# A transformer block on one core: the opening's layer-norm root taken from ScalarE, its first block worked in halves, and its splits in another order

## The chip, the cores and the metric

The kernel runs on one core of a Trainium2 chip. The core has a matrix engine (TensorE, PE in the profile, with its weight loads shown as PEld), a vector engine (VectorE, DVE), a scalar engine (ScalarE, ACT), GpSimd (POOL), and SyncE (SP), which issues most of the transfers. Each engine works through its own instructions in the order in which the program issues them; engines wait for one another through semaphores. The metric is the time of one execution on the device in microseconds.

## The reference

A pre-normed attention layer with 32 query heads on one shared key and value head, followed by a bilinear feed-forward layer, on 2048 rows of width 576 in float32:

```python
B, S, D, H = 1, 2048, 576, 32;  Dh = D // H          # Dh = 18, F = 4608
x = A_x
h = x + attention(_layernorm(x), wq, wk, wv, wo)      # softmax(q k^T * Dh**-0.5) v, then @ wo
n = _layernorm(h)
h2 = h + ((n @ w_gate) * (n @ w_up)) @ w_down         # no nonlinearity on either branch

def _layernorm(x, axis=-1, eps=1e-5):
    m = jnp.mean(x, axis=axis, keepdims=True)
    v = jnp.var(x, axis=axis, keepdims=True)
    return (x - m) / jnp.sqrt(v + eps)
```

## The kernel before

The 2048 rows are worked in four blocks of 512, each of four tiles of 128 rows. To come near float32, most products are made from a high and a low part of each operand: `split` casts a value to the matrix format on one engine (the high part, usually ScalarE, line 96) and subtracts the cast from the value on VectorE (the low part, line 97). A product is then three matmuls: high by high, low by high and high by low; `passes` lists them for the five 128-row slices of the width (the fifth holds the last 64 columns twice, its lower half the low part, so it needs two).

The program has three stages. The opening, `keys_values`, normalises all of x, transposes it, and projects keys and values. Then come score and value products of block 0 (`pair` and `flush`), with the query projections of all blocks between them, and at last the feed-forward layer of each block with the next block's attention dealt in between. The order of every engine's work is written out by hand; nothing is reordered by time.

The opening, in the order of its own names:

- `stats(lo, hi)` takes mean and variance of tiles lo to hi on VectorE (`ln_stats`, lines 111 and 112: two partial statistics and their union for a tile).
- `scale(lo, hi, eng)` makes 1/sqrt(variance + 1e-5) and the negative product of it and the mean. `rstd` (lines 121 to 133) starts from an integer estimate and makes three Newton steps; block 0 does it on VectorE, blocks 1 to 3 on GpSimd, where a step has one instruction more.
- `apply(b)` writes the normalised tiles xh of a block on ScalarE (line 194), four instructions.
- `twice(eng)` copies the last 64 columns of each xh beside themselves (line 199), on GpSimd for blocks 0 and 3 and on VectorE for blocks 1 and 2.
- `turn(b)` transposes on TensorE: two PSUM tiles tr of two row tiles each, and a tail.
- `parts()` splits what has been transposed into XT: a cast and a subtraction for each of the two tr, and for the tail.
- `project(b)` multiplies XT of a block by the joint weights w_h and w_l of keys, values and the last queries (14 matmuls, line 232). The raw weights wkv and wqr come by SP's queue behind block 0's x.
- `mean`, `keys` and `bound` make the keys' high and low part kk, their largest absolute value kabs and from it a bound on the scores, which replaces the maximum in the softmax; the bound, the queries and the keys pass through memory by SP's queue (lines 255, 276, 449, 534, 540).
- `queries(0)`, taken a step at a time as `first`, projects block 0's queries (line 407 and from line 416).

The first `pair` needs kT and the loads of q with its bound. From then on the loop of `run` alternates score products, one exponential instruction on ScalarE for each (line 611) and the value products.

Of the kernel before, what the change touches and what calls it, by code (L numbers as in the profile page):

```python
# [26 lines left out]
P = 128  # L27
# [3 lines left out]
NQ = TB // P  # L31
# [26 lines left out]
class Block:  # L58
# [84 lines left out]
    def keys_values(self):  # L143

        pe, act, dve, sp, pool = self.pe, self.act, self.dve, self.sp, self.nc.gpsimd
        p0 = self.op
# [23 lines left out]
        mv = p0.tile([P, NT, 2], F32, name="mv")  # L170
        nmean, kab, kabq = (p0.tile([P, 1], F32, name=n) for n in ("nmean", "kab", "kabq"))
        kabs = p0.tile([P, NB], F32, name="kabs")
        pool.memset(nmean, 0.0)
        pool.memset(kabs, 0.0)
        rs, xhs, trs, psks, tq_last = {}, {}, [], {}, []

        def stats(lo, hi):
            for j in range(lo, hi):
                b, s = divmod(j, NQ)
                self.ln_stats(xs[b][:, s, :], mv[:, j, :], s, f"a{b}")  # L180

        def scale(lo, hi, eng):
            r = self.rstd(mv[:, lo:hi, 1], f"a{lo}", eng, hi - lo)
            n = self.lp.tile([P, hi - lo], F32, tag="n", name=f"n{lo}")
            eng.tensor_tensor(n, mv[:, lo:hi, 0], r, ALU.mult)
            eng.tensor_scalar(n, n, -1.0, None, ALU.mult)
            for j in range(lo, hi):
                rs[j] = r[:, j - lo:j - lo + 1], n[:, j - lo:j - lo + 1]

        def apply(b):  # L190
            for s in range(NQ):
                xh = xhs[s] = self.p0q.tile([P, 640], F32, tag=f"wq{1 + s // 2}_{s % 2}", name=f"xh{b}_{s}")
                r, n = rs[NQ * b + s]
                act.activation(xh[:, 0:D], xs[b][:, s, :], AF.Identity, bias=n, scale=r)

        def twice(eng, lo=0, hi=NQ):

            for s in range(lo, hi):
                eng.tensor_copy(xhs[s][:, D:], xhs[s][:, 512:D])

        def turn(b):

            tail = self.ps_m(f"trt{b}")
            for r in range(2):
                tr = self.ps_s(f"tr{b}_{r}").rearrange("p a (c q) -> p (a c) q", q=2 * P)
                for s in (2 * r, 2 * r + 1):
                    for c in range(4):
                        pe.transpose(tr[:, c, (s - 2 * r) * P:(s - 2 * r + 1) * P],
                                     xhs[s][:, c * P:(c + 1) * P], self.ident)
                trs.append((b, r, tr))  # L210
                yield
            for s in range(NQ):
                pe.transpose(tail[:, s * P:(s + 1) * P], xhs[s][:, 512:], self.ident)
                del xhs[s]
            trs.append((b, None, tail))
            yield

        def parts():

            while trs:  # L220
                b, r, tr = trs.pop(0)
                XT = self.XT[b]
                if r is None:
                    self.split_tail(XT[:, 8, :], tr)
                else:
                    sl = slice(2 * r * P, (2 * r + 2) * P)
                    self.split(XT[:, 0:4, sl], XT[:, 4:8, sl], tr)

        def project(b):
            psk = psks[b] = (self.ps_f if b % 2 else self.ps_a)(f"psk{b}")  # L230
            for i, (w, m) in enumerate(passes(w_h, w_l, self.XT[b])):
                pe.matmul(psk, w, m, start=(i == 0), stop=(i == 13))

        def mean():

            act.activation(kv[:, 0:TB], psks[0], AF.Copy, accum_out=ksum)
            dve.tensor_scalar(nmean[R_K:], ksum[R_K:], -1.0 / TB, None, ALU.mult)

        def keys(b):


            sl = slice(b * TB, (b + 1) * TB)
            kk = self.pp.tile([P, 2, TB], F32R, tag="P", name=f"kk{b}")
            act.activation(kk[:, 0], psks[b], AF.Identity, bias=nmean)

            def highest():
                dve.tensor_reduce(kabs[R_K:, b:b + 1], f32(kk[R_K:, 0]), AX.X, ALU.max, apply_absolute_value=True)

            def low():
                if b:  # L250
                    dve.tensor_copy(kv[64:96, sl], psks[b][64:96])
                dve.scalar_tensor_tensor(kk[:, 1], psks[b], nmean, f32(kk[:, 0]), ALU.add, ALU.subtract)
                del psks[b]
                for j, k in enumerate((0, 0, 1)):
                    sp.dma_start(f32(self.kT[j:3 * DH:3, sl]), f32(kk[R_K:R_K + DH, k]))
                if b:
                    store()
                    again(b)

            def store():  # L260
                rows = self.q_dram[b, HL * DH:]
                sp.dma_start(rows[:, 0:2, :], f32(kk[:R_V]))
                sp.dma_start(rows[:, 2, :], f32(kk[:R_V, 0]))

            def queries():
                if not b:
                    store()
                tq = self.qb.tile([P, TB], F32R, tag="tq", bufs=5, name=f"tql{b}")
                dve.scalar_tensor_tensor(tq[:R_V], f32(kk[:R_V, 0]), -1.0, f32(kk[:R_V, 0]), ALU.mult, ALU.max)
                tq_last.append(tq)  # L270
            return highest, low, queries
# [18 lines left out]

        first = self.queries(0)

        act.copy(w_h, wkv)
# [5 lines left out]
        pool.tensor_tensor(w_l, wkv, f32(w_h), ALU.subtract)  # L299
# [1246 lines left out]
def rows(b, c):  # L1546

    return 7 * DH if b == 0 and c < 4 else P


def drain(gen):
    for _ in gen:
        pass
# [85 lines left out]
```

## Time and profile before

| what | value |
|---|---|
| median of 3 runs | 2285.42 us (2283.07 to 2285.66) |
| profiled execution | 2286.16 us, of which the span from the first to the last instruction is 2284.4 us |
| mean granted TensorE clock | 0.999 |
| TensorE matmuls busy | 2250.6 us, 99% of the span |
| ScalarE busy | 1510.1 us, 66% |
| VectorE busy | 1272.1 us, 56% |
| GpSimd busy | 726.6 us, 32% |
| first score matmul starts | 47.62 us |

A row of the order of time gives the start, the length, the engine, the line of the code, the operation and its tiles, how many instructions were merged, and in brackets how long the engine had stood idle before it and what ended that. A row of the groups gives the line, engine, operation and shapes, the count, then busy time in total and the mean of one in nanoseconds, then the idle time before them with its releasers. The rows of the stretches are explained where they stand.

### The profile page before, as it was taken

The page shows a single profiled execution, that of the slowest core. Times are in us where ns is not written, and L with a number is a line of the kernel's source. Part 1 is how long each engine was busy: PE and PEld are TensorE (multiplying, and loading weights), DVE is VectorE, ACT ScalarE, POOL GpSimd, SP SyncE. Part 2 cuts the span into 40 slices and gives each one's busy share as a digit, 9 for nine tenths or more (in the row PEclk, how much of TensorE's full clock was granted, in tenths as well). Part 3 has the DMA queues.
Part 4 walks back from the last instruction along what each step waited for, and adds up shares of the span by engine and source line. Part 5 has one row for each costly group of instructions (what it writes and reads, how often), then busy time and mean ns, then how long its engine had stood idle before and what let it go on. Part 6 is the DMA issues. An engine that isn't in the chain of part 4 may idle for free.

```text
span 2284.4 us, 46386 instructions
## 1 busy us (share of the span) xinstructions
PE 2250.6 (99%) x17958; PEld 1635.1 (72%) x17958; DVE 1272.1 (56%) x2190; ACT 1510.1 (66%) x2052; POOL 726.6 (32%) x848
## 2 busy tenths in 40 slices
PE   7999999999999999999999999999999999999999
PEld 5333334777777777777777777767777788999999
DVE  7655635444445446454544455544444477778776
ACT  5889877767776766667676767567676724555553
POOL 5445401323333333233333333322222244222222
PEclk9999999999999999999999999999999999999999
DMA  5778853545555554645555544654343345677775
GB/s 172 232 257 294 274 195 96 160 150 164 170 168 162 169 173 142 202 155 171 163 168 167 161 163 153 193 183 138 118 128 101 106 165 172 207 244 237 233 248 171
DMA packets 199271, 407.05 MB, mean 178 GB/s; under 512 B 21342, under 2 KB 53214, under 8 KB 199046
## 3 DMA queue, kind: packets, MB, share of 16 engines
q1 hardware_dynamic: 196309, 392.78, 53.6%
q0 software_dynamic: 2736, 11.26, 1.6%
q8 instruction: 143, 2.34, 0.4%
q14 instruction: 83, 0.67, 0.1%
HBM read 317.27 MB, written 74.55 MB: 172 GB/s over the span
## 4 chain that ended last, share of the span: by engine, by line
PE 82%; DVE 1%; ACT 1%; issue 1%; POOL 1%; DMA 0%; SPq 0%; ACTq 0%; POOLq 0%; DVEq 0%
PE pg L945 22%; PE acc L615 15%; PE y L897 13%; PE s L610 9%; PE gs L1161 8%; PE yq L1126 4%; PE pu L945 3%; PE yo L741 3%; PE gu L945 2%; PE gs L1168 2%; PE y L867 1%; ACT P L611 0%; DMA out_dram<-h 0%; POOL h L908 0%; DVE ws L97 0%
## 5 line engine op out<-in xcount | busy, mean ns | idle before, releaser
L611 ACT ACTIVATE P<-s 128x1024 f32<-128x1024 f32 x1024 | 1025.6, 1027 | 277.0 <-PE s L610 198.4
L945 PE MATMUL pu<-X,ws 64*128 64x512 f32 x2565 | 694.2, 389 | 0.0
L945 PE MATMUL pg<-X,ws 64*128 64x512 f32 x2565 | 693.1, 389 | 0.1
L945 PEld LDWEIGHTS pg<-X,ws 64*128 64x128 f32 x2565 | 475.1, 185 | 70.7 <-DMA wsum<-in_wgs_dram 0.8
L615 PE MATMUL acc<-P,V 128*32 128x512 f32 x4096 | 491.3, 599 | 0.7 <-ACT P L611 0.6
L945 PEld LDWEIGHTS pu<-X,ws 64*128 64x128 f32 x2565 | 472.4, 185 | 6.9 <-ACT tmp L874 0.3
L610 PE MATMUL s<-q,kT 56*128 56x512 f32 x2048 | 443.2, 422 | 7.2 <-ACT P L611 3.7
L908 POOL TENSOR_TENSOR h<-h,tmp 128x288 f32<-128x288 f32 x306 | 238.5, 806 | 597.8 <-ACT tmp L907 596.3
L610 PEld LDWEIGHTS s<-q,kT 56*128 56x128 f32 x2048 | 201.1, 184 | 207.4 <-ACT P L611 119.8
L897 PEld LDWEIGHTS y<-wdo,room 128*128 128x128 f32 x2142 | 289.8, 188 | 43.2 <-issue 34.8
L897 PE MATMUL y<-wdo,room 128*128 128x288 f32 x2142 | 303.8, 300 | 1.3 <-DVE h L903 1.2
L615 PEld LDWEIGHTS acc<-P,V 128*32 128x32 f32 x4096 | 114.5, 109 | 247.0 <-issue 236.2
L903 DVE TENSOR_TENSOR h<-h,y 128x288 f32<-128x288 f32 x408 | 175.8, 452 | 200.5 <-PE y L897 200.3
L907 ACT COPY tmp<-y 128x288 f32<-128x288 f32 x306 | 122.0, 399 | 241.4 <-PE y L897 219.0
L976 DVE TENSOR_TENSOR hf<-pu,g 128x512 f32<-128x512 f32 x95 | 65.7, 691 | 302.6 <-ACT g L972 302.6
L96 POOL CAST ws<-wr 128x1152 fp32r<-128x1152 f32 x108 | 127.0, 1176 | 315.0 <-PE pu L945 244.7
L97 DVE TENSOR_TENSOR ws<-wr,ws 128x1152 fp32r<-128x1152 f32 x108 | 185.2, 1715 | 64.6 <-POOL ws L96 61.8
L1109 POOL TENSOR_TENSOR wsum<-wsum,wsum 128x512 f32<-128x512 f32 x72 | 99.4, 1381 | 137.8 <-DMA wsum<-in_wgs_dram 137.7
L97 DVE TENSOR_TENSOR room<-S,room 128x1024 fp32r<-128x1024 f32 x51 | 62.5, 1226 | 132.1 <-ACT room L96 132.1
L1126 PE MATMUL yq<-wdo,XW 128*128 128x288 f32 x504 | 86.0, 297 | 0.1
L945 PE MATMUL gu<-X,ws 64*128 64x512 f32 x702 | 82.0, 389 | 0.0
L748 DVE TENSOR_TENSOR h<-h,yo 128x288 f32<-128x288 f32 x154 | 63.3, 452 | 32.3 <-PE yo L741 28.5
(257 smaller groups left out, 2638.6 us busy)
## 6 DMA issues: line engine op xcount, KB each, us to landing
wdo<-wd_dram SPq DMA_DIRECT2D x492, 288.0 KB
wr<-in_wgu_dram SPq DMA_DIRECT2D x108, 576.0 KB
wsum<-in_wgs_dram SPq DMA_DIRECT2D x108, 256.0 KB
wd_dram<-wd_room SPq DMA_DIRECT2D x20, 1008.0 KB
wsum_dram<-wsum SPq DMA_DIRECT2D x72, 256.0 KB
raw<-wsum_dram SPq DMA_DIRECT2D x72, 256.0 KB
q<-q_dram SPq DMA_DIRECT2D x64, 216.0 KB
raw<-in_wgs_dram SPq DMA_DIRECT2D x54, 256.0 KB
```

The lines of the kernel that those rows point to most:

```text
L96: (copy or self.cast)(hi, src)
L97: self.dve.tensor_tensor(lo, src, f32(hi), ALU.subtract)
L610: self.pe.matmul(s_[:, i], self.kT[o:o + 56, t * P:(t + 1) * P], q[o:o + 56, pr], start=True, stop=True)
L611: self.act.activation(p_, s_, AF.Exp, scale=SCALE)
L615: self.pe.matmul(acc[32 * j:32 * j + 32, :], self.V[:, t, :], Ps[j // 2][:, j % 2, :], start=(t == 0), stop=(t == NT - 1), skip_group_chec ...
L897: pe.matmul(y[:, :HD], m[:, t * P:(t + 1) * P], k, start=(first and j == 0), stop=(j == 2), skip_group_check=True)
L903: dve.tensor_tensor(hs, hs, y[:, :HD], ALU.add)
L907: act.copy(z, y[:, :HD])
L908: pool.tensor_tensor(hs, hs, z, ALU.add)
L945: pe.matmul(ps, w[o:o + 64, wk, c], X[o:o + 64, xk, c], start=(j == 0), stop=(j == 26))
L1126: pe.matmul(y[:, :HD], A[:, k, x, t * P:(t + 1) * P], v[:, l], start=(first and z == j == 0), stop=(z == len(pairs) - 1 and j == 2), skip_ ...
L1161: pe.matmul(bank[:, g * HT:(g + 1) * HT], W[:, wk, c, g], X[:, 2 * xk + c], start=(first and g == c == wk == xk == 0), stop=(c == 1 and wk ...
```

## The change

Only the opening is changed, and the order of the matmuls inside a key projection.

- **The root.** The integer estimate and three Newton steps give way to a square root of variance + eps on ScalarE (`root`), a reciprocal of it on VectorE and one Newton step on the engine that did the work before (VectorE for block 0, GpSimd for the others). On VectorE a chain has six instructions, on GpSimd seven beside VectorE's reciprocal. A constant tile eps is set on GpSimd. After the keys of block 2, one Exp of that tile is issued on ScalarE.
- **Halves.** Block 0 takes statistics, root and scale for tiles 0 and 1, then for tiles 2 and 3; tile 0 is applied before the second root, the other three after it.
- **The weights.** w_h is cast and w_l subtracted on GpSimd; the cast of the first query weights moves on ScalarE behind block 0's casts.
- **Low parts.** `high` and `low` take the cast and the subtraction of a tr apart, so that they stand in another order among roots and reciprocals.
- **Copies.** The tail copies of blocks 1 and 2 move from VectorE to GpSimd.
- **Order.** Statistics of blocks 1 to 3 are taken at other places; `highs_first` puts the products with the high part of XT ahead of those with its low part.

```diff
+        eps = p0.tile([P, 1], F32, name="eps")
+        pool.memset(eps, 1e-5)
...
+        def root(lo, hi):
+            g = roots[lo] = self.lp.tile([P, NQ], F32, tag="g", name=f"g{lo}")[:, :hi - lo]
+            act.activation(g, mv[:, lo:hi, 1], AF.Sqrt, bias=eps)
+            return g
+
         def scale(lo, hi, eng):
-            r = self.rstd(mv[:, lo:hi, 1], f"a{lo}", eng, hi - lo)
...
+            g = roots.pop(lo)
+            eng.tensor_scalar(v, mv[:, lo:hi, 1], 1e-5, -0.5, ALU.add, ALU.mult)
+            dve.reciprocal(g, g)
+            eng.tensor_tensor(t, g, g, ALU.mult)
+            eng.tensor_tensor(t, t, v, ALU.mult)
+            if eng is dve:
+                eng.scalar_tensor_tensor(y, t, 1.5, g, ALU.add, ALU.mult)
+                eng.scalar_tensor_tensor(n, mv[:, lo:hi, 0], -1.0, y, ALU.mult, ALU.mult)
+            else:
+                eng.tensor_scalar(t, t, 1.5, None, ALU.add)
+                eng.tensor_tensor(y, t, g, ALU.mult)
+                eng.tensor_tensor(n, mv[:, lo:hi, 0], y, ALU.mult)
+                eng.tensor_scalar(n, n, -1.0, None, ALU.mult)
...
+        def high():
+            b, r, tr = trs[0]
+            self.cast(self.XT[b][:, 0:4, 2 * r * P:(2 * r + 2) * P], tr)
+            lows.append(trs.pop(0))
+
+        def low():
+            b, r, tr = lows.pop()
+            XT, sl = self.XT[b], slice(2 * r * P, (2 * r + 2) * P)
+            dve.tensor_tensor(XT[:, 4:8, sl], tr, f32(XT[:, 0:4, sl]), ALU.subtract)
...
-            for i, (w, m) in enumerate(passes(w_h, w_l, self.XT[b])):
+            for i, (w, m) in enumerate(highs_first(passes(w_h, w_l, self.XT[b]))):
...
-        act.copy(w_h, wkv)
+        stats(0, 2)
+        root(0, 2)
+        stats(2, 3)
+        scale(0, 2, dve)
+        stats(3, 4)
+        apply(0, 0, 1)
+        root(2, 4)
+        scale(2, 4, dve)
+        apply(0, 1)
+        self.split_pool(w_h, w_l, wkv)
+        twice(pool)
+        stats(4, 8)
+        drain(turn(0))
+        high()
+        low()
+        high()
+        root(4, 8)
+        scale(4, 8, pool)
+        low()
+        parts()
         act.copy(self.wq[0][0], wqr)
-        stats(0, 4)
-        scale(0, 4, dve)
-        apply(0)
-        twice(pool, 0, 1)
-        pool.tensor_tensor(w_l, wkv, f32(w_h), ALU.subtract)
-        twice(pool, 1)
-        stats(4, 8)
-        scale(4, 8, pool)
         pool.tensor_tensor(self.wq[0][1], wqr, f32(self.wq[0][0]), ALU.subtract)
-        drain(turn(0))
-        parts()
         stats(8, 12)
-        scale(8, 12, pool)
         project(0)
         apply(1)
-        stats(12, 13)
-        twice(dve)
+        twice(pool)
         drain(turn(1))
-        stats(13, 16)
-        scale(12, 16, pool)
+        high()
+        root(8, 12)
+        scale(8, 12, pool)
+        low()
         for _ in range(14):
             next(first)
         parts()
         mean()
+        stats(12, 16)
         apply(2)
-        twice(dve)
+        twice(pool)
         drain(turn(2))
         next(first)
...
         project(1)
+        high()
+        root(12, 16)
+        scale(12, 16, pool)
+        low()
         parts()
...
         high2, low2, queries2 = keys(2)
+        act.activation(eps, eps, AF.Exp)
...
+def highs_first(p):
+    return p[0:12:3] + p[2:12:3] + p[1:12:3] + p[12:]
```

More of the change, by code (lines that the diff above doesn't have):

```diff
@@ L180, in stats, with apply @@
                 self.ln_stats(xs[b][:, s, :], mv[:, j, :], s, f"a{b}")
+        def root(lo, hi):
+            g = roots[lo] = self.lp.tile([P, NQ], F32, tag="g", name=f"g{lo}")[:, :hi - lo]
+            act.activation(g, mv[:, lo:hi, 1], AF.Sqrt, bias=eps)
+            return g
         def scale(lo, hi, eng):
-            r = self.rstd(mv[:, lo:hi, 1], f"a{lo}", eng, hi - lo)
-            n = self.lp.tile([P, hi - lo], F32, tag="n", name=f"n{lo}")
-            eng.tensor_tensor(n, mv[:, lo:hi, 0], r, ALU.mult)
-            eng.tensor_scalar(n, n, -1.0, None, ALU.mult)
+            v, t, y, n = (self.lp.tile([P, NQ], F32, tag=k, name=f"{k}a{lo}")[:, :hi - lo] for k in "vtyn")
+            g = roots.pop(lo)
[11 more added lines that the diff above has]
+                eng.tensor_scalar(n, n, -1.0, None, ALU.mult)
             for j in range(lo, hi):
-                rs[j] = r[:, j - lo:j - lo + 1], n[:, j - lo:j - lo + 1]
-        def apply(b):
-            for s in range(NQ):
+                rs[j] = y[:, j - lo:j - lo + 1], n[:, j - lo:j - lo + 1]
+        def apply(b, lo=0, hi=NQ):
+            for s in range(lo, hi):
                 xh = xhs[s] = self.p0q.tile([P, 640], F32, tag=f"wq{1 + s // 2}_{s % 2}", name=f"xh{b}_{s}")
```

1 line of the change is left out of this document (added).

## The prediction

> **What bounds the kernel now.** I read the stretches first, then VectorE's and ScalarE's orders of time in the opening, then the groups of the first 60 us. In the stretches the columns are start:end and length, then busy time of TensorE, its weight loads, VectorE, ScalarE and GpSimd, with the granted clock behind them.
>
> ```profile
> 18.00:28.00 10.00, 9.31 (x47) 6.78 (x46) 9.41 (x31) 6.61 (x10) 6.87 (x27) 1.00 0.02 4
> ...
> 48.00:60.00 12.00, 10.94 (x65) 5.88 (x65) 7.87 (x15) 7.18 (x8) 6.04 (x7) 0.86 0.60 182
> ...
> 120.00:220.00 100.00, 99.80 (x736) 38.26 (x732) 58.76 (x68) 89.18 (x93) 49.38 (x56) 1.00 0.79 267
> ```
>
> From 120 us on TensorE is busy 99.80 of 100 us, and its order there is untouched. A gain in the opening can only move that stretch forward; it cannot grow in it. So the whole question is how much earlier the first score matmul starts. In the opening VectorE is the queue that never rests (9.41 of 10 us), and the rows below are its turning points.
>
> ```profile
> 3.77 0.82 DVE L111 BATCH_NORM_STATS2 bsa<-x 128x6 f32<-128x288 f32 x2 [3.77 <-DMA x<-in_x_dram]
> ...
> 8.09 0.17 DVE L121 TENSOR_SCALAR va<-mv 128x4 f32<-128x4 f32 x1
> ...
> 10.67 0.17 DVE L186 TENSOR_SCALAR n<-n 128x4 f32<-128x4 f32 x1
> 10.75 0.81 DVE L111 BATCH_NORM_STATS2 bsa<-x 128x6 f32<-128x288 f32 x2
> 10.88 3.15 ACT L194 ACTIVATE xh<-x,n,ya 128x576 f32<-128x576 f32 x4 [0.94 <-DVE n L186]
> ...
> 14.37 0.21 DVE L112 BATCH_NORM_AGGREGATE mv<-bsa 128x2 f32<-128x12 f32 x1
> 14.95 1.23 DVE L97 TENSOR_TENSOR XT<-tr,XT 128x1024 fp32r<-128x1024 f32 x1 [0.36 <-ACT XT L96]
> ...
> 17.72 0.69 DVE L106 TENSOR_TENSOR XT<-trt,XT 64x512 fp32r<-64x512 f32 x1
> ...
> 31.06 0.69 DVE L97 TENSOR_TENSOR qs<-psq,qs 126x512 fp32r<-126x512 f32 x1 [0.27 <-ACT qs L96]
> ...
> 35.37 0.68 DVE L247 TENSOR_REDUCE kabs<-kk 32x1 f32<-32x512 f32 x1
> 36.53 0.16 DVE L281 COPY kabq<-psb 128x1 f32<-128x1 f32 x1 [0.48 <-PE psb L280]
> ```
>
> And what leads from there to the first score matmul:
>
> ```profile
> 38.12 2.50 SPq L255 DMA_DIRECT2D kT<-kk  x3
> ...
> 44.62 0.73 SPq L276 DMA_DIRECT2D kT<-kT  x1
> 45.41 0.72 SPq L540 DMA_DIRECT2D q<-m_dram  x2
> ...
> 46.77 0.69 ACT L244 ACTIVATE kk<-psk,nmean 128x512 fp32r<-128x512 f32 x1 [4.46 <-PE psk L232]
> ...
> 47.62 0.99 PE L610 MATMUL s<-q,kT 56*128 56x512 f32 x4 [0.88 <-DMA q<-m_dram]
> ```
>
> The first pair waits for a transfer, not for TensorE: the lowest VectorE result of block 0's keys goes to kT at 38.12, its copy is issued at 44.62, the two bound loads at 45.41, and TensorE idles 0.88 us until they land. So a microsecond saved in VectorE's queue before 36.5 us is a microsecond saved at 47.62, and TensorE's own chain has 0.88 us of slack there.
>
> **The change part by part.** The prices:
>
> ```profile
> L111 DVE BATCH_NORM_STATS2 bsa<-x 128x6 f32<-128x288 f32 x32 | 12.6, 434 | 4.0 <-DMA x<-in_x_dram 4.0
> L97 DVE TENSOR_TENSOR XT<-tr,XT 128x1024 fp32r<-128x1024 f32 x8 | 9.5, 1218 | 0.7 <-ACT XT L96 0.7
> L199 POOL COPY xh<-xh 128x64 f32<-128x64 f32 x8 | 1.8, 235 | 9.9 <-ACT xh L194 9.8
> L199 DVE COPY xh<-xh 128x64 f32<-128x64 f32 x8 | 1.2, 188 | 0.4 <-POOL ta L127 0.3
> L293 ACT ACT_TABLE_LOAD x1 | 1.3, 1283 | 0.8 <-PEq L1627 0.8
> L236 ACT ACTIVATION_READ_ACCUMULATOR kvw<-psk 128x1 f32 x1 | 0.2, 205 | 0.0
> L194 ACT ACTIVATE xh<-x,n,ya 128x576 f32<-128x576 f32 x16 | 12.6, 861 | 5.4 <-POOL n L186 4.5 <-DVE n L186 0.9
> L96 ACT CAST XT<-tr 128x1024 fp32r<-128x1024 f32 x8 | 7.7, 1003 | 0.5 <-PE tr L208 0.5
> L661 DVE RECIPROCAL rc<-os 128x16 f32<-128x16 f32 x24 | 5.9, 245 | 0.0
> ```
>
> *The root on VectorE.* Block 0's chain of 15 small instructions runs from 8.09 to 10.67 + 0.17 = 10.84: 2.75 us, 0.184 each. It becomes two chains of six for half a block each: 12 x 0.184 = 2.2 us. *The roots of blocks 1 to 3* stay on GpSimd but hand one reciprocal each to VectorE: the nearest row is 245 ns for 16 columns, other four-column rows take 0.17, so I take 0.2, three times: 0.6 us (0.5 to 0.7). On GpSimd 18 instructions become seven, of which six come after the reciprocal.
>
> ```profile
> 14.67 0.22 POOL L121 TENSOR_SCALAR va<-mv 128x4 f32<-128x4 f32 x1 [0.36 <-DVE mv L112]
> ...
> 19.43 0.23 POOL L186 TENSOR_SCALAR n<-n 128x4 f32<-128x4 f32 x1
> ```
>
> These 18 took 19.66 - 14.67 = 4.99 us, 0.277 each, so six take 1.7 us. In exchange the chain of block b now starts only when its reciprocal's turn comes on VectorE.
>
> *The five square roots* are new on ScalarE, two to four columns each. Nothing like them is in the trace; between 205 ns (a one-column read) and 861 ns (576 columns) I take 0.3, nearest the one-column row. Statistics of tile 2 hide the first. The reciprocal of tiles 2 and 3 must wait for the second, behind the 0.86 us of the first xh: 0.2 us or so. The third is ready while VectorE subtracts. The fourth (block 2) is late: with block 0's second half done at 11.2 (below), block 1's statistics (10.75 to 14.58 now, 3.83) end at 15.05, a subtraction of 1.2 and the reciprocal at 16.5, GpSimd's part at 18.2, four xh (3.15) at 21.35, a cast of block 1 (1.0) at 22.3 and the root at 22.6; VectorE has meanwhile done block 0's other two subtractions (1.2, and 0.69 for the half-height one) and block 2's statistics (3.83) by 22.1, and waits 0.5 us. The fifth is hidden by VectorE's two query instructions (0.69 for the first).
>
> *Copies of the tail* leave VectorE in blocks 1 and 2: 1.2 us less. On GpSimd they take 0.235 each behind the xh, in idle time.
>
> *VectorE's waits.* It idles 0.7 us for ScalarE's casts, 0.4 at its copies, 0.3 more for a query cast and 0.2 for x: about 1.4 in blocks 0 to 2 that the new order (xh earlier, each cast ahead of its subtraction) should close.
>
> *The weight split on GpSimd.* This puts a 1.54 us subtraction where GpSimd was idle. Three kinds of rows tell what that does to a VectorE instruction with both inputs in SBUF:
>
> ```profile
> 12.09 1.54 POOL L299 TENSOR_TENSOR w_l<-kvw,w_h 128x640 fp32r<-128x640 f32 x1
> 31.66 0.68 DVE L428 SCALAR_TENSOR_TENSOR tq<-qs 126x512 fp32r<-126x512 f32 x1
> 31.79 0.62 POOL L131 TENSOR_TENSOR ya<-ta,ya 128x4 f32<-128x4 f32 x1
> 45.26 1.45 POOL L101 TENSOR_TENSOR wq<-wqr,wq 128x630 fp32r<-128x630 f32 x1
> 45.40 1.86 DVE L269 SCALAR_TENSOR_TENSOR tql<-kk 72x512 fp32r<-72x512 f32 x1
> 8.17 0.72 ACT L293 CAST w_h<-kvw 128x640 fp32r<-128x640 f32 x1 [6.09 <-DMA kvw<-in_wkv_dram]
> ```
>
> At 45.40 a VectorE product that takes 0.68 at 31.66 took 1.86: it ended 0.55 us after GpSimd's subtraction (45.26 + 1.45 = 46.71). At 31.79 a four-column GpSimd instruction ended at 32.41, just behind VectorE's at 32.34. Whichever starts second waits for the first. In the new order wkv lands at 8.17, GpSimd casts to about 8.9 (ScalarE's 0.72 taken for it) and subtracts to about 10.5. VectorE's first half-chain (6.8 to 8.0) is clear of it, but the second half's g*g is due at about 9.65: held until 10.5, 0.85 us. The bounds are 0 (the small instructions slip in) and 1.6 (the first half is late too and meets the cast). I take 0.85. No row shows a small VectorE instruction held by a long GpSimd one, and with no hold the sum below would be -1.7 instead of -0.8. The Trainium skill, "SBUF — State Buffer", section "Who interferes with whom", has no size in its rule: a VectorE instruction with two SBUF inputs contends with a GpSimd instruction that reads SBUF, and the later one blocks fully; by it the whole hold comes, and the two large cases above agree.
>
> *Casts, copies and orders on ScalarE and TensorE.* The cast of w_h leaves ScalarE; the cast of wq moves behind block 0's casts (0.72 us, covered: its first reader is the query matmul past 21 us; uncovered it costs 0.7). The orders with high parts first let the key projections start before the low parts are there; TensorE has slack at 47.62, so they count nothing. The extra table load for Exp, 1.28 us, and its small Exp stand in ScalarE's 4.46 us idle ahead of the last kk (46.77); bare it would cost 1.3 to 1.6. The memset of eps (0.1) sits in front of GpSimd's idle time. No transfer is added or passes another on SP's or GpSimd's queue; GpSimd's one load of query weights still follows block 3's tail copies.
>
> *The sum at VectorE's kabs reduction* (ends at 36.05 now): -2.75 + 2.2 + 0.6 - 1.2 - 1.4 + 0.2 + 0.5 + 0.85 = -1.0 us. The keys' low part behind it also needs a TensorE product queued behind the transposes of block 3's first two tiles, and those start only after the reciprocal, 1.7 us of GpSimd and two xh: that takes back 0.2. So the first pair starts 0.8 us earlier, at about 46.8. Behind it everything is in order and moves along: 2286.16 (the profiled execution: span 2284.4 and 1.76 around it) becomes 2285.4. That execution lies 0.74 above the median of the three runs, so against 2285.42 I forecast **2284.6**.
>
> **The rivals.** *The split does not hold VectorE, and the slow clock is missed.* After the first pairs the clock falls:
>
> ```profile
> 50.00:51.00 1.00, 1.00 (x4) 0.75 (x3) 0.99 (x2) 0.35 (x1) 0.13 (x1) 0.50 0.67 193
> ...
> 41.42 1.80 PE L407 MATMUL psq<-XT,wq 128*126 128x512 f32 x7
> ...
> 49.15 3.24 PE L407 MATMUL psq<-XT,wq 128*126 128x512 f32 x7
> ```
>
> At 0.50 seven query matmuls take 3.24 instead of 1.80: 1.4 us. Earlier work may or may not fall in such a window. With -1.7 for the opening this gives 2285.4 - 3.1 = 2282.3. For it: the second half's instructions have two columns only. Against it: the row at 31.79 is as small and was held.
>
> *The gain is used up on the way.* If the first half-chain is late by 0.2 us it meets the cast, the hold grows to 1.6, the fourth root costs its 0.86 instead of 0.3, and the first pair comes 0.5 later than now: 2285.9. For it: two handovers between engines replace one engine's own chain. Against: VectorE has less to do.
>
> *Slower: the tables change with each root.* If xh's function and the casts were not in the square root's table, each of the four later roots would bring two loads of 1.283 us on ScalarE. Four uncovered loads cost 5.1, all eight 10.3; in the middle 7.7 - 0.8 gives 2292.3. It decides from five uncovered loads (6.4 - 0.8 = 5.6, over 0.2%). For it: one load stands in the trace, and no row shows a square root beside the others. Against it: that one load at the start serves copies, the scaled apply and every Exp. The Trainium skill, "ScalarE: Activation LUTs", section "Table sets: the hidden batching unit", says that identity and copy are in every set, by which only two loads would show; no row here shows it.
>
> **How the numbers follow.** A difference under 0.2% (4.6 us) is about what a measurement of this kernel can tell from no change. Forecast: 0.48. Split harmless and clock luck: 0.24, of it 0.06 with more than 4.6 us, if all of VectorE's waits go too (another 1.5). Gain used up: 0.18, of it 0.03 past 4.6 us if further slow windows fall on later work. Tables: 0.06. Left over: 0.04 faster for something not seen. So faster 0.10, same 0.81, slower 0.09. The range goes from 2281.6 (rival one and a little) to 2287.3 (rival two with one more slow window, 1.4).
>
> **What would show it.** In the changed kernel: exactly two table loads, the second in ScalarE's idle time before the last kk; the last xh of block 0 ending at about 13.1 (14.03 now), or at 12.1 with no hold; VectorE's second g*g stretched to about 1 us beside the w_l subtraction; the wait before block 2's reciprocal at about 0.5; first score matmul at 46.8 with its wait still for the bound loads. Two more table loads, a first pair past 47.6, or one before 45.5, would make the forecast wrong.

## The result, and the profile after

The changed kernel takes 2293.23 us (median of 6 runs, 2289.00 to 2298.28); the kernel before takes 2283.51 us beside it (6 runs, 2282.94 to 2285.66). The ratio is 1.0041, with a 95% interval from 1.0030 to 1.0051: 9.7 us slower, where 2284.6 was forecast and 2287.3 was the upper end of the range. The profiled execution of the changed kernel took 2298.28 us, its span is 2296.5 us and its mean granted clock 0.995 (before: 2286.16, 2284.4 and 0.999).

First the stretches of the changed kernel, with the columns of the prediction's table (busy time of TensorE, weight loads, VectorE, ScalarE, GpSimd, then the granted clock).

```profile
18.00:28.00 10.00, 9.68 (x57) 7.47 (x57) 9.29 (x25) 9.71 (x15) 5.04 (x17) 1.00 0.01 3
28.00:38.00 10.00, 8.09 (x43) 6.79 (x42) 7.86 (x17) 7.03 (x11) 2.40 (x11) 0.83 0.35 123
48.00:60.00 12.00, 10.13 (x57) 4.99 (x57) 8.17 (x16) 6.91 (x8) 7.89 (x9) 0.78 0.64 205
120.00:220.00 100.00, 99.80 (x740) 38.51 (x732) 56.14 (x67) 89.53 (x94) 48.88 (x56) 1.00 0.80 266
```

Up to 220 us nothing here costs ten microseconds: from 120 us on TensorE is busy 99.80 of 100 us, as before. The rows of the opening in order of time, changed kernel, answer to the turning points of the prediction:

```profile
5.74 1.28 ACT L188 ACT_TABLE_LOAD   x1 [5.74 <-DVE mv L112]
...
7.03 0.29 ACT L188 ACTIVATE g<-mv,eps 128x2 f32<-128x2 f32 x1
...
9.05 1.54 POOL L101 TENSOR_TENSOR w_l<-kvw,w_h 128x640 fp32r<-128x640 f32 x1
...
9.31 1.30 DVE L195 TENSOR_SCALAR va<-mv 128x2 f32<-128x2 f32 x1
...
11.58 1.62 ACT L214 ACTIVATE xh<-x,na,ya 128x576 f32<-128x576 f32 x2 [1.22 <-DVE na L201]
...
22.54 0.18 DVE L196 RECIPROCAL g<-g 128x4 f32<-128x4 f32 x1 [0.36 <-ACT g L188]
...
33.98 1.87 PE L228 MATMUL tr<-C,xh 128*128 128x128 f32 x8 [1.91 <-ACT xh L214]
...
34.27 0.68 DVE L279 TENSOR_REDUCE kabs<-kk 32x1 f32<-32x512 f32 x1
...
36.11 0.16 DVE L313 COPY kabq<-psb 128x1 f32<-128x1 f32 x1 [1.15 <-PE psb L312]
...
42.55 1.28 ACT L402 ACT_TABLE_LOAD   x1
...
42.98 0.53 SPq L587 DMA_DIRECT2D q<-m_dram  x2
...
46.74 0.40 PE L264 MATMUL psk<-XT,w_l 128*128 128x512 f32 x1
47.07 0.73 PE L657 MATMUL s<-q,kT 56*128 56x512 f32 x4
47.17 0.69 ACT L276 ACTIVATE kk<-psk,nmean 128x512 fp32r<-128x512 f32 x1 [3.12 <-PE psk L264]
```

The opening did roughly what was said of it: two table loads, the last xh of block 0 at 13.20, kabs ready at 34.95 (36.05 before), the first score matmul at 47.07 (47.62 before). So the loss lies behind the opening. To place it, the starts of the 1024 exponentials on ScalarE are compared one by one, since their order is the same in both kernels (difference of the changed kernel to the one before, the first being number 0):

| exponential | its start before, us | changed minus before, us |
|---|---|---|
| 0 | 48.4 | -0.65 |
| 10 | 65.6 | +3.4 |
| 200 | 274.8 | +3.2 |
| 250 | 335.4 | +4.7 |
| 1020 | 1815.7 | +13.7 |

The steps of 4.0 us (up to number 10) and 1.5 us (200 to 250) go with stretches at half the granted clock. The profile of the kernel before has two of them, 3.4 us each, from 49.3 and from 305.3 us; this execution of the changed kernel has longer ones:

```profile
54.80:68.40 13.60, 13.19 (x51) 4.22 (x51) 5.42 (x8) 6.89 (x8) 7.45 (x8) 0.50 0.64 201
308.00:313.00 5.00, 5.00 (x24) 0.90 (x20) 4.03 (x4) 3.64 (x4) 4.68 (x5) 0.50 0.98 351
```

The remaining 9.0 us, about the whole difference of the medians, grow evenly from 335 to 1816 us, and there the granted clock is 1.00. The same 1400 us of both kernels in the view of stretches, the kernel before first:

```profile
400.00:1800.00 1400.00, 1398.19 (x11532) 1017.46 (x11530) 676.55 (x1132) 959.47 (x1239) 432.82 (x460) 1.00 0.50 158
```

```profile
400.00:1800.00 1400.00, 1398.06 (x11466) 996.59 (x11466) 673.56 (x1128) 956.56 (x1233) 427.55 (x453) 1.00 0.50 158
```

TensorE is busy 1398 us in both, at full clock, and issues 66 matmuls fewer: at 1400/11532 = 0.121 us each that is 8.0 us. TensorE waits for nothing more than before; it is slower. The groups tell which matmuls, first of the kernel before, then of the changed one (busy time, mean ns of one):

```profile
L945 PE MATMUL pu<-X,ws 64*128 64x512 f32 x2565 | 694.2, 389 | 0.0
L945 PE MATMUL pg<-X,ws 64*128 64x512 f32 x2565 | 693.1, 389 | 0.1
```

```profile
L992 PE MATMUL pu<-X,ws 64*128 64x512 f32 x2565 | 705.1, 393 | 0.0
L992 PE MATMUL pg<-X,ws 64*128 64x512 f32 x2565 | 704.8, 393 | 0.1
...
L992 PE MATMUL gu<-X,ws 64*128 64x512 f32 x702 | 82.0, 389 | 0.0
```

The feed-forward's gate and up products take 393 ns instead of 389. That is 22.6 us of busy time; since several matmuls are in flight at once, it makes less in elapsed time. The group gu, the same kind of matmul with the same operands, still takes 389; it runs from 1828 to 1956 us, behind the last score product (1818).

The diff touches no line of the feed-forward. It does add tiles, though: eps (32 bytes of each partition, with its rounding) in the pool "o", and the tag g (two buffers of 32 bytes) in the layer norm's pool. Pools lie one behind the other, so every later tile moves. By the addresses of the two built programs, the residual tiles h, q and P stand 64 bytes further on, and oT, X, the feed-forward's weights ws and all behind them 96 bytes. The keys kT and the values V lie ahead of these pools and stay.

### The profile page after: what moved, and what is told of

It reads as the page before. It is cut to its first block, busy times and chain, and to the rows that moved or that the text cites. A ratio compares the mean times of both kernels' runs of the same rounds, so it can differ in the third digit from the quotient of the medians.

```text
span 2296.5 us, 46370 instructions
## 1 busy us (share of the span) xinstructions
PE 2265.2 (99%) x17958; PEld 1622.2 (71%) x17958; DVE 1267.0 (55%) x2182; ACT 1511.8 (66%) x2058; POOL 722.1 (31%) x825
## 4 chain that ended last, share of the span: by engine, by line
PE 82%; DVE 2%; DMA 1%; ACT 1%; issue 0%; POOL 0%; SPq 0%; ACTq 0%; POOLq 0%; DVEq 0%
PE pg L992 22%; PE acc L662 15%; PE y L944 13%; PE s L657 9%; PE gs L1208 8%; PE yq L1173 4%; PE pu L992 4%; PE yo L788 3%; PE gu L992 2%; PE gs L1215 1%; PE y L914 1%; DMA q<-q_dram 1%; ACT P L658 0%; DVE ws L97 0%; POOL h L955 0%
## 5 line engine op out<-in xcount | busy, mean ns | idle before, releaser
L992 PE MATMUL pu<-X,ws 64*128 64x512 f32 x2565 | 705.1, 393 | 0.0
L992 PE MATMUL pg<-X,ws 64*128 64x512 f32 x2565 | 704.8, 393 | 0.1
L657 PE MATMUL s<-q,kT 56*128 56x512 f32 x2048 | 437.9, 423 | 5.9 <-ACT P L658 3.3
```

What stands on the lines that cost most here:

```text
L657: self.pe.matmul(s_[:, i], self.kT[o:o + 56, t * P:(t + 1) * P], q[o:o + 56, pr], start=True, stop=True)
L992: pe.matmul(ps, w[o:o + 64, wk, c], X[o:o + 64, xk, c], start=(j == 0), stop=(j == 26))
```

## The experiments

My theory after this: the places of the tiles in SBUF slow the feed-forward, and the new order has nothing to do with it. The rival: the new order leaves something behind (another phase of transfers or of clock) that slows it. For each run I give the time, the mean of pg, and the drift, by which I mean how much the distance from exponential 250 to 1020 grew against the kernel before (9.0 us in the changed kernel). The drift leaves out the opening and its half-clock stretches.

### The tiles without the change

The kernel before, with the new tiles made and set once but never used; all else as it was.

```diff
+        eps = p0.tile([P, 1], F32, name="eps")
+        pool.memset(eps, 1e-5)
+        for i in range(2):
+            pool.memset(self.lp.tile([P, NQ], F32, tag="g", name=f"g{i}"), 1.0)
         pool.memset(nmean, 0.0)
```

> The kernel before, with nothing changed but the eps tile and the two g tiles of the change allocated and set once on GpSimd, so that every later tile lies as many bytes further as in the changed kernel (64 for P, q and h, 96 for X, ws and what follows). Placement theory (the feed-forward's matmuls are slower where their tiles now lie; the changed kernel lost 9 us evenly between 400 and 1830 us at a granted clock of 1.00): 5 to 9 us slower than the kernel before, with the loss spread evenly over the feed-forward blocks. Clock theory (all of the loss comes from half-clock windows that the new opening brings): no change, 2283.5. Opening theory (a later first pair): no change.

Measured: 2293.44 us (5 runs) against 2284.72 (21 runs), ratio 1.0037 with an interval from 1.0024 to 1.0051; drift 8.75 us.

```profile
L949 PE MATMUL pu<-X,ws 64*128 64x512 f32 x2565 | 705.1, 393 | 0.0
```

The new tiles alone make the whole loss. Each of them alone:

```diff
+        eps = p0.tile([P, 1], F32, name="eps")
+        pool.memset(eps, 1e-5)
```

> The kernel before with the eps tile alone: P, q and h stay, X, ws and what follows lie 32 bytes further, at a multiple of 64. Placement theory with alignment to 64 bytes as its rule: as slow as with both tiles, 5 to 9 us. Placement theory with the distance of P as its rule: no change. Clock and opening theories: no change, 2283.5.

```diff
+        for i in range(2):
+            pool.memset(self.lp.tile([P, NQ], F32, tag="g", name=f"g{i}"), 1.0)
```

> The kernel before with the two g tiles alone: everything lies 64 bytes further, so every tile keeps its place within 64 bytes. Placement theory with alignment to 64 bytes as its rule: no change, 2283.5. Placement theory with P's or q's distance as its rule: 5 to 9 us slower. Clock and opening theories: no change.

With eps alone (what lies behind it moves by 32 bytes; P, q and h stay): ratio 1.0023 (1.0014 to 1.0032, 11 runs), drift 4.7 us, 391 ns. With g alone (everything behind the layer norm's pool moves by 64): ratio 1.0043 (1.0030 to 1.0057, 5 runs), drift 10.4 us, 392 to 393 ns. A move by a full 64 bytes costs no less than one by 32, so a rounding to 64 bytes is not the rule.

### The change without its displacement

The changed kernel, with eps in one tile with nmean and g in the buffers of an old tag, so that h, q, P, X and ws stand where they stood:

```diff
-        nmean, kab, kabq = (p0.tile([P, 1], F32, name=n) for n in ("nmean", "kab", "kabq"))
+        kab, kabq = (p0.tile([P, 1], F32, name=n) for n in ("kab", "kabq"))
+        ne = p0.tile([P, 2], F32, name="nmean")
+        nmean, eps = ne[:, 0:1], ne[:, 1:2]
...
-        eps = p0.tile([P, 1], F32, name="eps")
...
-            g = roots[lo] = self.lp.tile([P, NQ], F32, tag="g", name=f"g{lo}")[:, :hi - lo]
+            g = roots[lo] = self.lp.tile([P, NQ], F32, tag="yi", name=f"g{lo}")[:, :hi - lo]
```

> The changed kernel with its eps laid beside nmean and its g in the tag of the integer estimate, so that X, ws, P, q and h lie where they lay before; its instructions and their order are unchanged. Placement theory: the even loss is gone, 2283 to 2288, the rest being half-clock windows (0 to 6 us) less about 0.7 us for the earlier first pair. Clock theory: 2289 to 2294 as the changed kernel.

Measured: 2284.66 us (11 runs) against 2284.72, ratio 1.0001 (0.9992 to 1.0010). The drift is 0.0 us.

```profile
L993 PE MATMUL pu<-X,ws 64*128 64x512 f32 x2565 | 693.7, 389 | 0.0
L993 PE MATMUL pg<-X,ws 64*128 64x512 f32 x2565 | 693.0, 389 | 0.1
```

With this the rival is out: the whole new order runs at the old pace once the tiles are back. What the order itself is worth, the measurement cannot tell from nothing.

### Which tile

All tiles of one side of a boundary are moved by 64 bytes, in the kernel before. First X and all that lies behind it in the pool w and in the pools that follow (X's view starts 64 bytes into an enlarged tile), then the same with X left in place:

```diff
-                X = self.X = self.wp.tile([P, 2, 9, TB], F32R, tag="X", bufs=1, name=f"X{b}")
+                X = self.wp.tile([P, 18 * TB + 16], F32R, tag="X", bufs=1, name=f"X{b}")
+                X = self.X = X[:, 16:].rearrange("p (k c q) -> p k c q", k=2, c=9)
```

> The kernel before with X moved by 64 bytes inside a larger tile, and with it all behind X in the pool w (raw weights, down weights, ws), the pool hid and P2; P, q, h and oT stay. The mean of a feed-forward matmul (pg<-X,ws) tells: 389 ns in the kernel before, 391 to 393 in the three moved kernels. If the place of X or ws by itself sets it: 391 to 393, and 5 to 10 us lost between 400 and 1830 us. If the place of P or q sets it: 389, no loss.

```diff
-                X = self.X = self.wp.tile([P, 2, 9, TB], F32R, tag="X", bufs=1, name=f"X{b}")
+                X = self.wp.tile([P, 18 * TB + 16], F32R, tag="X", bufs=1, name=f"X{b}")
+                X = self.X = X[:, 0:18 * TB].rearrange("p (k c q) -> p k c q", k=2, c=9)
```

> The kernel before with X where it was, and all behind it in w, hid and P2 moved by 64 bytes. If the place of X sets it: 389 ns, no loss. If the place of ws sets it: 391 to 393 ns and 5 to 10 us. If only the distance of X and ws sets it: 391 to 393 here and 389 where both move together.

Then h, q and P alone (the tiles g added, and three small tiles of "o" joined in one, which frees the same 64 bytes, so that all behind P stays), and the opposite, everything behind P:

```diff
-        nmean, kab, kabq = (p0.tile([P, 1], F32, name=n) for n in ("nmean", "kab", "kabq"))
+        nkk = p0.tile([P, 3], F32, name="nmean")
+        nmean, kab, kabq = (nkk[:, i:i + 1] for i in range(3))
...
+        for i in range(2):
+            pool.memset(self.lp.tile([P, NQ], F32, tag="g", name=f"g{i}"), 1.0)
```

> The kernel before with h, q, P and ob moved by 64 bytes (the g tiles) and all behind at its old place (nmean, kab and kabq share one tile). If the place of P or q sets it: 391 to 393 ns and 5 to 10 us. If that of X or ws: 389, no loss.

```diff
+        pool.memset(p0.tile([P, 1], F32, name="pad0"), 0.0)
+        pool.memset(p0.tile([P, 1], F32, name="pad1"), 0.0)
```

> The kernel before with P, q and h at their places and all behind (os, oT, w, hid, P2) moved by 64 bytes. If the place of X or ws sets it: 391 to 393 ns and 5 to 10 us. If P's place: 389. If the distance of P to X and ws sets it, the two kernels that move only one of them are both slow, and with both moved by 64 (as in the run with the g tiles alone) it would not have been slow, which it was.

All four are slow; one execution each, beside 2283.53 us for the kernel before. Times and drifts: 2290.41 and 6.7 us (X and behind), 2289.81 and 8.2 (behind X), 2286.87 and 5.9 (h, q, P), 2290.60 and 6.0 (behind P). No one group is to blame: whichever moves, the pace falls. One row differs; moved by 64 bytes, X together with its weights, and below it the weights without X:

```profile
L946 PE MATMUL gu<-X,ws 64*128 64x512 f32 x702 | 82.0, 389 | 0.0
```

```profile
L946 PE MATMUL pu<-X,ws 64*128 64x512 f32 x2565 | 702.1, 392 | 0.0
L946 PE MATMUL pg<-X,ws 64*128 64x512 f32 x2565 | 701.7, 392 | 0.1
L946 PE MATMUL gu<-X,ws 64*128 64x512 f32 x702 | 84.0, 395 | 0.0
```

The matmuls gu slow down only where the weights move against X. That points to the distance between tiles, not to the place of one.

### Distances and sizes

If distances count, moving everything together must cost nothing; and the size of a move may have a period. First everything by 64 bytes, the constants, kT and V included; then everything behind kT and V by 128 and by 256 bytes:

```diff
+            self.pad = cp.tile([P, 16], F32, name="pad")
             self.C = cp.tile([P, C_W], F32, name="C")
...
+        pool.memset(self.pad, 0.0)
```

> The kernel before, with a tile of 64 bytes put ahead of everything else: the constants, kT, V and every later tile stand 64 bytes further on, and all of them keep their places relative to each other. If only the places of the tiles to each other matter: feed-forward matmuls of 389 ns, no drift against the kernel before (under 1.5 us between the 250th and the 1020th exp), time 2282 to 2286 us. If the addresses themselves matter, or the place against something below the tiles: 391 to 393 ns, 4 to 11 us of drift, 2287 to 2296 us.

```diff
+        for i in range(2):
+            pool.memset(self.lp.tile([P, 16], F32, tag="pad", name=f"pad{i}"), 0.0)
```

> The kernel before, with 128 bytes of unused tile in the layer norm's pool: kT, V and the other constants unmoved, everything behind 128 bytes further on. If any change of the distance to kT and V costs, whatever its size: 391 to 393 ns and 2287 to 2296 us. If only displacements that are no multiple of 128 bytes cost: 389 ns and 2282 to 2286 us.

```diff
+        for i in range(2):
+            pool.memset(self.lp.tile([P, 32], F32, tag="pad", name=f"pad{i}"), 0.0)
```

> As the run with 128 bytes, with 256 bytes. If the cost has a period of 256 bytes or less: 389 ns and 2282 to 2286 us. If the places of before are merely a lucky set among many: 391 to 393 ns again, 2287 to 2296 us.

The group pu of the three, in this order (the kernel before ran in 2284.5 us beside them, 15 runs):

```profile
L946 PE MATMUL pu<-X,ws 64*128 64x512 f32 x2565 | 693.9, 389 | 0.0
```

```profile
L947 PE MATMUL pu<-X,ws 64*128 64x512 f32 x2565 | 701.7, 392 | 0.0
```

```profile
L947 PE MATMUL pu<-X,ws 64*128 64x512 f32 x2565 | 694.2, 389 | 0.0
```

Everything together by 64 bytes: 2286.21 us (0.2 above the range expected), drift 0.35. Behind kT and V by 128: 2295.84 us, drift 7.2. By 256: 2285.46 us, drift 0.2. So it is the distance that counts, and as far as these sizes go it counts modulo 256 bytes: moves by 32, 64 and 128 cost, and so does the changed kernel's 64 and 96, while 0 and 256 do not. A larger multiple was not tried.

### One tile alone

With that period a single tile can be moved by 64 bytes while all behind it moves by a harmless 256:

```diff
-            self.kT = cp.tile([P, S], F32R, name="kT")
+            self.kT = cp.tile([P, S + 64], F32R, name="kT")[:, 16:16 + S]
```

> The kernel before with kT alone moved by 64 bytes against the rest (64 bytes of pad in front of it and 192 behind, so that everything behind it moves by 256, which cost nothing). If what counts is the keys' place against the moving operand X of the feed-forward matmuls: 391 to 393 ns. If kT has no part in it: 389 ns and 2282 to 2287 us.

```diff
-            self.V = cp.tile([P, NT, 32], F32, name="V")
+            self.V = cp.tile([P, NT * 32 + 64], F32, name="V")[:, 16:16 + NT * 32].rearrange("p (n d) -> p n d", n=NT)
```

> The same for V alone: 391 to 393 ns for the feed-forward matmuls if V's place against X (or against the feed-forward's weights) counts, 389 ns and 2282 to 2287 us if not.

```diff
-                X = self.X = self.wp.tile([P, 2, 9, TB], F32R, tag="X", bufs=1, name=f"X{b}")
+                X = self.wp.tile([P, 18 * TB + 64], F32R, tag="X", bufs=1, name=f"X{b}")
+                X = self.X = X[:, 16:16 + 18 * TB].rearrange("p (k c q) -> p k c q", k=2, c=9)
```

> The same for X alone, whose own weights, and everything else behind it, move by 256. If the place of X against its own weights ws counts for the matmuls that run without attention between them (gu): these go from 389 to 395 ns, as with the weights alone moved, and pg and pu to 391 to 393. If it was the weights' place against something else: gu stays at 389.

The groups with kT alone moved, V alone, X alone (the kernel before: 2284.08 us, 15 runs):

```profile
L945 PE MATMUL pu<-X,ws 64*128 64x512 f32 x2565 | 705.2, 393 | 0.0
```

```profile
L945 PE MATMUL pu<-X,ws 64*128 64x512 f32 x2565 | 693.8, 389 | 0.0
```

```profile
L946 PE MATMUL pu<-X,ws 64*128 64x512 f32 x2565 | 702.9, 392 | 0.0
...
L946 PE MATMUL gu<-X,ws 64*128 64x512 f32 x702 | 82.6, 391 | 0.0
```

kT: 2298.48 us, drift 11.6, the largest of all. V: 2286.77 us, drift 0.2. X: 2296.57 us, drift 7.4, and gu at 391, not at the 395 that I expected (here the weights come 64 bytes nearer to X, there they stood 64 further; whether that is the reason was not tried). The keys are no operand of the matmuls that slow down. Between 400 and 1800 us TensorE reads them as the stationary operand of the score matmuls (line 610), which are dealt in between the feed-forward's; no other instruction of that stretch reads or writes them. The values do not count; none of their products stands next to a product of pg or pu there.

A reading near at hand is that a weight load of kT or ws, fetched while another matmul streams X, q or P, is slowed or slows the stream when the two lie badly to each other. The starts in the traces speak against it. Between 400 and 1800 us the usual cycle is a pair of score matmuls and then four pairs of pg and pu. The medians over 512 cycles of the kernel before, 519 of the changed one and 517 with kT alone moved, in ns:

| from one start to the next | before | changed | kT alone moved |
|---|---|---|---|
| score pair to first pair pg, pu | 229 | 234 | 239 |
| first to second | 229 | 237 | 235 |
| second to third | 227 | 240 | 233 |
| third to fourth | 227 | 235 | 235 |
| fourth to the next score pair | 235 | 230 | 233 |
| whole cycle | 1147 | 1173 | 1175 |

In all three the loads of kT's weights start with the fourth pair. So with kT alone moved that reading would slow only the last step, and it is the only step that did not slow. In the three steps from the first pair to the fourth the records show only X streamed and ws loaded; these two had kept their places to each other, and yet each step took 6 to 8 ns more. What collides stays open. That the distance of kT to the rest sets the pace is measured.

### The cure by 256 bytes, and VectorE's hold

The changed kernel with eps beside nmean as above, and its tiles g of 128 bytes each, so that everything behind the layer norm's pool moves by 256 bytes:

```diff
-            g = roots[lo] = self.lp.tile([P, NQ], F32, tag="g", name=f"g{lo}")[:, :hi - lo]
+            g = roots[lo] = self.lp.tile([P, 32], F32, tag="g", name=f"g{lo}")[:, :hi - lo]
```

> The changed kernel with the tile eps beside nmean and with the tiles g of 128 bytes each instead of 32, so that everything behind the layer norm's pool stands 256 bytes further on than before instead of 64 to 96. If only the displacement modulo 256 bytes costs: 389 ns, ratio to before 0.9992 to 1.0010, as with the old places. If the new tile itself costs: 391 to 393 ns and a ratio of 1.002 to 1.005.

Measured: 2285.56 us (11 runs) against 2284.08 (15), ratio 1.0006 (0.9997 to 1.0015), drift 0.4 us. Its 1400 us in the view of stretches:

```profile
400.00:1800.00 1400.00, 1397.99 (x11529) 1016.85 (x11528) 676.29 (x1132) 958.93 (x1238) 431.37 (x460) 1.00 0.50 158
```

11529 matmuls, three short of the 11532 before, against 11466 in the changed kernel as it was.

The last experiment is on the opening: the changed kernel at the old places, with GpSimd's subtraction for w_l behind block 0's tail copies.

```diff
-        self.split_pool(w_h, w_l, wkv)
+        pool.tensor_copy(w_h, wkv)
         twice(pool)
+        pool.tensor_tensor(w_l, wkv, f32(w_h), ALU.subtract)
         stats(4, 8)
```

> The changed kernel with its tiles at the places of before, and with GpSimd's subtraction for w_l moved behind the tail copies of block 0, so that nothing long runs on GpSimd beside VectorE's second half-chain. If GpSimd's subtraction was what stretched the small VectorE instruction to 1.30 us: no instruction of the two half-chains is longer than 0.3 us, the last xh of block 0 ends about 1.1 us earlier, at 12.1. If VectorE waited there for something else: it still lasts about 1.3 us and xh ends at 13.2. On the time: if a microsecond saved on VectorE in the opening reaches the end, the ratio to before is 0.9990 to 0.9998 (0.5 to 2 us faster); if the opening's gains are lost to the granted clock's half-speed stretches, 0.9995 to 1.0008.

```profile
9.46 0.22 DVE L196 TENSOR_SCALAR va<-mv 128x2 f32<-128x2 f32 x1
...
10.77 1.62 ACT L215 ACTIVATE xh<-x,na,ya 128x576 f32<-128x576 f32 x2 [0.26 <-DVE na L202]
...
12.75 1.53 POOL L337 TENSOR_TENSOR w_l<-kvw,w_h 128x640 fp32r<-128x640 f32 x1
...
46.22 0.39 PE L265 MATMUL psk<-XT,w_l 128*128 128x512 f32 x1
46.54 0.72 PE L659 MATMUL s<-q,kT 56*128 56x512 f32 x4
```

The instruction that lasted 1.30 us now lasts 0.22, so it was GpSimd's subtraction that held it, and xh ends at 12.39, 0.8 us earlier (12.1 was expected). The time does not follow: 2285.08 us against 2284.5, ratio 1.0005 (0.9995 to 1.0015). The first score matmul starts at 46.54, directly behind TensorE's own products, without a wait.

## Why the prediction was wrong

**The step that failed** is the sentence "Behind it everything is in order and moves along", with the one it rests on, that a gain in the opening can only move the later stretch forward. The order is the same, but not the pace: the same instructions ran on tiles at other addresses, at 393 instead of 389 ns, and a difference in pace grows over the whole length, 9.0 us from 335 to 1816 us. I had costed the new tile eps by its memset alone, and the places of eps and g at nothing. No rival had this mechanism; the only one whose time lay more than 0.2% on the slower side was the tables, with a chance of 0.06. That its 2292.3 came near the measured 2293.23 is chance, since no further table load came.

**The sum at kabs** held: 1.0 us was forecast, 36.05 - 34.95 = 1.1 measured. Of its terms, the roots took 0.29 us (0.3 taken), the reciprocals 0.17 to 0.18 (0.2), the fourth root's wait was 0.36 (0.5). The last xh of block 0 ended at 13.20 (13.1). VectorE's idle time from its first instruction to kabs fell from 2.74 to 2.09 us (2.39 in the changed kernel at the old places), where the sum had 0.7 less (-1.4 + 0.2 + 0.5); the waits that the sum listed for the 1.4 add up to 1.6. The other profiles bear the gain out: kabs is ready between 35.87 and 36.79 in the 14 with the old opening, and at 34.95, 35.08 and 35.45 in the three that run the changed order as it was. An agreement to 0.1 us is finer than that spread.

**The hold** came. In the changed kernel it fell on another instruction than predicted, the scaling ahead of the reciprocal: 9.31 to 10.61, 1.1 us longer than the 0.22 without the subtraction, against 0.85 for g*g. In the same order of instructions at the old places it fell on g*g, 1.08 us instead of 0.16:

```profile
9.46 0.17 DVE L196 TENSOR_SCALAR va<-mv 128x2 f32<-128x2 f32 x1
9.79 0.17 DVE L197 RECIPROCAL g<-g 128x2 f32<-128x2 f32 x1 [0.16 <-ACT g L189]
9.99 1.08 DVE L198 TENSOR_TENSOR ta<-g 128x2 f32<-128x2 f32 x1
```

There GpSimd's subtraction ran from 9.51 to 11.05, so the scaling had started just ahead of it, and in the changed kernel just behind it (9.31 against 9.05). The reciprocal, one input, ran beside it in its usual 0.17. The rule of the Trainium skill, "SBUF — State Buffer", "Who interferes with whom", spoke of two inputs in SBUF, and g*g agrees; the scaling has one tensor input there. The same section names such scalings among the operations that can take the ports shared with GpSimd in a faster mode, where their operands allow it; the row agrees with that in so far as it ended 0.02 us after the subtraction (9.05 + 1.54 = 10.59).

**From kabs to the first pair** the size came out near (0.55 us earlier in the profile, 0.8 forecast), but by luck. The prediction let TensorE's 0.88 us of slack stand and let the transfer of the bound set the time. The bound loads were indeed issued 2.43 us earlier (42.98 instead of 45.41), but the pair did not follow them: it stands directly behind the last psk, with no idle time in its row. That is no work of the change alone. Of the 14 profiles with the old opening only five show a wait before the first pair; in the other nine it stands directly behind the last psk too, here with the tiles g alone:

```profile
46.49 0.40 PE L234 MATMUL psk<-XT,w_l 128*128 128x512 f32 x1
46.81 0.86 PE L612 MATMUL s<-q,kT 56*128 56x512 f32 x4
```

So which of the two ends last changes from execution to execution, and the prediction read one execution as the rule. The first pair starts between 46.45 and 48.81 in those 14, and between 46.17 and 47.38 in the four with the new opening; 0.55 us between one of each says little. Part of TensorE's lateness is new: in all four it runs ahead with the high parts and then waits 1.9 us for xh (in the changed kernel 1.91 from 32.07). In three of the four the clock falls to half for 3.4 us behind that gap, from 34.32, 35.12 and 35.89; none of the 14 with the old opening has such a stretch ahead of 49.3. In the fourth, the changed kernel at the old places, the gap was the same and the clock stayed (second fence), and its first pair is the earliest of the 18, at 46.17. Another gap of 1.93 us, between 300 and 308 us, is in all 18 profiles; in ten a half-clock stretch begins around its end, in eight none does. So such a gap alone does not bring the slow clock, but it may well be a part of what does; no run closed one.

```profile
34.00:36.00 2.00, 2.00 (x11) 1.68 (x12) 0.92 (x2) 2.00 (x3) 0.70 (x3) 0.58 0.07 20
```

```profile
34.00:36.00 2.00, 1.80 (x14) 1.50 (x14) 1.35 (x4) 2.00 (x4) 0.71 (x3) 1.00 0.08 29
```

**The tables**: exactly two loads, the second in ScalarE's idle time ahead of the last kk, which still idles 3.12 us behind it. This rival is out, and the Trainium skill's "ScalarE: Activation LUTs", "Table sets: the hidden batching unit", agrees for identity and copies.

**The half-clock stretches** were priced at 1.4 us, by one group of matmuls. They weigh more. At exponential 10 the profiles of the 13 other kernels with the old opening lie between 3.9 us earlier and 3.1 us later than the profile before, and those of the four with the new opening between 0.8 earlier and 3.4 later. A gain below one microsecond at the first pair cannot be followed through that. With the tiles at their old places or 256 bytes on, the ratios to before are 1.0001, 1.0005 and 1.0006, each interval holding 1: no change that can be measured. A gain of 0.8 us, a ratio of 0.9996, is too small for these runs to confirm or to refuse; nothing in them shows that it reached the end.

## What to carry to other kernels

Here a new tile of 32 bytes moved every tile behind it, and on a kernel that TensorE bounds the distances between its operands can be worth more than a microsecond of instructions: compare the mean of the large matmul groups and the count of matmuls in a stretch at full clock before looking for a lost wait. Put a small helper tile into the slot of an old one, or make it move the rest by 256 bytes; here either brought all of the 9 us back. And when a chain in front of a wait gets shorter, look at what the waiting engine itself still has queued, in more than one execution: the wait of 0.88 us that this forecast was built on was missing in nine of the 14 profiles with that opening.

## What the runs showed of the hardware

- The pace of the matmuls pg and pu depends on the distances of tiles in SBUF: 389 ns at the old distances, 391 to 393 after moves by 32, 64 or 128 bytes, 389 after 256; gu took up to 395. Over the 250th to the 1020th exponential that makes 4.7 to 11.6 us.
- The place of one group's stationary operand sets the pace of another group: kT moved by 64 bytes slowed the products of X and ws (for pg 693 to 705 us), also in steps in which no weights of kT are loaded; V moved by 64 bytes did not. The Trainium skill's "SBUF — State Buffer", "Who interferes with whom", gives TensorE two read ports, independent of each other, and holds that only the pair shared by VectorE and GpSimd contends; by that alone no move of a tile would change TensorE's pace, and the measurement shows that one does. What collides inside is open.
- A VectorE scaling of two columns, 0.22 us by itself, lasted 1.30 us beside a GpSimd subtraction; a product of two columns, 0.16 by itself, 1.08; a reciprocal that started during such a subtraction took its usual 0.17.
- The granted clock stood at 0.50 for 13.6 us (54.8 to 68.4) while TensorE was busy 13.19 of them. A half-clock stretch of 3.4 us followed an idle gap of 1.9 us in three profiles of four, and did not in the fourth.
